# Second halves of the output sums under the slot rule, and another order at the start, in a kernel that mixes full and dilated local attention

## The chip, the cores and the metric

The kernel runs on one core of a Trainium2 chip. A core has five engines that run side by side and wait for each other on semaphores: TensorE (PE in the profile; its weight loads are PEld), VectorE (DVE), ScalarE (ACT), GpSimd (POOL) and SyncE (SP), which issues most of the transfers. The metric is the device time in microseconds (us). Before the change the median of nine runs is 851.13 us (850.04 to 852.61).

## The reference

The input x has 2048 rows of 512 numbers. Two attentions of 32 heads, 16 numbers a head, work on the same x and are mixed row by row with a gate:

```
g = sigmoid((x * gate_w).sum(-1))
A: p = softmax(q k^T / 4) over all 2048 keys;   a = (p v) @ A_wo
B: 8 keys per row, at distances 0, 2, ..., 14;  b = (softmax(q . k_w / 4) v_w) @ B_wo
out = g * a + (1 - g) * b
```

q, k and v are slices of x @ A_wqkv for A and of x @ B_wqkv for B. All in- and outputs are bf16.

## The kernel before

The work of A is cut into 32 periods, each of four heads (there are 8 groups i) and 512 queries (4 chunks c_). The list `periods` sets their order. A period has 64 units: for each of the four heads, 16 blocks of 128 keys. A unit is a score block of 128 keys by 512 queries, its exponential, and its share of the attention sums (PV). The four heads of a group sit in four strips of 32 rows, so up to four score matmuls run side by side on TensorE, and up to four PV matmuls in four strips of 32 columns.

Most units go through ScalarE. `act_stream` (L972) fills two rings in PSUM in turn, one of three score blocks and one of two, and `act_tail` (L953) takes the exponential of a whole ring in one instruction, from `ring` to `pT`. Such a ring's matmuls are called a score set here. A set can be filled again only when ScalarE has read it. Some units, called riders (`rider`, L1063), are computed elsewhere: their score block goes to one of two PSUM banks named w (`P.resource("w", 2)`, L450), and VectorE makes the exponential in four passes (ta, ta, ta, pd), or GpSimd does with psc after a copy by VectorE. `pv_job` (L892) adds the units to `acc`.

Everything else on TensorE is a job that needs a w bank: keys, queries, values, B's projections (`bw`), and the output sums. `final_job` (L1301) makes one tile of 128 output rows from eight matmuls: four with `oT` and `awo` for A, and four with `obt` and `bwo` for B, as two steps of four with the same bank (L1322; in the last chunk three, one and three). The first step has the job's priority, 30 and up, the second has `GO` = 1.9 (L471). Behind the second, VectorE copies the bank to `osb`, and SP stores it. The last of a chunk's four tiles sets `ev_final`.

No scheduler decides on the chip. The class `Plan` runs through the whole kernel once while it is built, with a cost for each step, and records the instructions in the order in which it gives them out; each engine then works through its own list. In `run` (L222) the ready step of the lowest priority number comes next on its engine. For TensorE three rules bear on the change:

- `fits` (L216): a step of priority 2 or more is held back, in steps of 0.1 us, unless its planned end lies before `limit` (L185), the planned time at which ScalarE runs out of work, less `refill` = 0.52. A step under 2 isn't asked.
- `room_for_job` (L200) and `rider` compare the work that VectorE has ahead with `JW` = 0.8: a job opens a bank only when VectorE has that much or the job has waited for 3.0 (`JP`), and riders stand back behind waiting jobs when it has more.
- `idle_fill` (L150) puts matmuls on zeros into gaps that the plan sees on TensorE (`z` by `ident` in the profile; written over a scratch bank, or added to `acc` as zeros), so that a share of 0.80 of each 3.4133 us is streamed. `stream` is told a step's length less 0.11 (L284). `SW` = 0.11 (L469) is the planned cost of going from one group of matmuls to another, `MM` = 0.2135 that of one matmul of 512 columns.

The start is in the same plan. Five transfers on SP's queue bring x (`load_x`, L395 to L403), in the order of the queue: rows 0 to 511, 512 to 1023, 1024 to 1535, and twice 256. Behind them the weights `wqr` of the first queries follow; the planned landings are `XARR` and `WARR` (L482, L483). Each quarter of x is transposed on TensorE in two halves (`x_half`, L540) and copied out by VectorE or ScalarE. `k_job` (L567) makes the keys of one quarter with four matmuls; for the first group the largest absolute key is taken by VectorE straight from the bank (`kmax_all`), and ScalarE writes the keys with a bias. `sel_job` (L598) takes the maximum of the four columns of `kmax_all` and makes the matrix `selk_all` from it. `q_job` (L750) makes the queries of a period; VectorE takes |q| (`absq`), one more matmul by `selk_all` adds a bound on the scores, and VectorE writes `qt`. Then the first score set can run. For the first period `q_job` waits for the third quarter of x (L754), though it reads the first.

## Time and profile before

| | us |
|---|---|
| median of nine runs | 851.13 |
| the profiled execution, its own time | 851.45 |
| its span, first to last instruction | 849.7 |
| TensorE busy | 758.0 |
| VectorE busy | 765.6 |
| ScalarE busy | 826.4 |
| GpSimd busy | 725.5 |
| ScalarE waiting for score sets, PE ring, 6 times | 5.1 |
| ScalarE waiting for PE acc (5 times) and PE w (3 times) | 1.6 + 1.1 |
| first exponential of a ring begins | 17.99 |
| last score set begins | 838.5 |

A row of the groups has the line, the engine, the operation, the tile written and the tile read with their shapes, the count, then the busy time in us and the mean of one in ns, and last the engine's idle time ahead of the group, with what ended it. Almost all rows name L347, the helper that records an instruction, so groups are told apart by their tiles. In a timeline a row begins with the start and the length in us; several equal instructions in succession are one row. In the table by stretches, each engine's busy time has its number of instructions behind it, and the granted TensorE clock, the DMA share and GB/s follow.

### The profile page before, as it was taken

What the parts mean: (1) busy time and instruction counts of PE and PEld (TensorE: products, weight loads), DVE (VectorE), ACT (ScalarE), POOL (GpSimd) and SP (SyncE); (2) the same over time, 40 slices, a digit from 0 to 9 for tenths busy, and PEclk for the clock granted to TensorE, in tenths of its full rate; (3) what the DMA queues carried; (4) which work ended last, traced back from release to release, by engine and by line L of the source; (5) the groups of instructions that cost most, each with busy time, mean ns of one, the idle gap of its engine ahead of it and who ended that gap; (6) DMA issues with size and microseconds to landing.
All of it is one profiled execution on the core that took longest, in us unless ns stands there. A gap on an engine that the chain in (4) does not pass through costs nothing.

```text
span 849.7 us, 15781 instructions
## 1 busy us (share of the span) xinstructions
PE 758.0 (89%) x5864; PEld 267.8 (32%) x5864; DVE 765.6 (90%) x1332; ACT 826.4 (97%) x748; POOL 725.5 (85%) x734
## 2 busy tenths in 40 slices
PE   9999999989998888888998988888898998888887
PEld 4432343333323332222333233333223223223222
DVE  5698889899999898998999899999989899999896
ACT  5999999999999999999999999999999999999996
POOL 2596886999799999899999999999899999997781
PEclk9999999999999999999999999999999999999999
DMA  9002304421444041303132414120313221201000
GB/s 295 5 14 88 100 27 140 152 64 39 129 119 162 32 127 29 112 13 105 33 93 66 124 43 130 45 94 7 106 32 112 87 81 26 63 13 57 14 1 26
DMA packets 72589, 63.84 MB, mean 75 GB/s; under 512 B 20528, under 2 KB 69168, under 8 KB 72512
## 3 DMA queue, kind: packets, MB, share of 16 engines
q1 hardware_dynamic: 71312, 62.57, 24.3%
q8 instruction: 46, 0.75, 0.4%
q10 hardware_dynamic: 1200, 0.26, 0.2%
q14 instruction: 31, 0.25, 0.1%
HBM read 46.14 MB, written 12.62 MB: 69 GB/s over the span
## 4 chain that ended last, share of the span: by engine, by line
ACT 66%; issue 20%; PE 13%; DVE 1%; POOL 0%; ACTq 0%; POOLq 0%
ACT pT L347 65%; PE w L347 5%; PE ring L347 3%; PE acc L347 3%; ACT lg L347 1%; PE s L347 1%; DVE ta L347 0%; PE e L347 0%; DVE pd L347 0%; DVE qpk L347 0%; DVE osb L347 0%; DVE kvs L347 0%; ACT osc L347 0%; ACT e L347 0%; DVE mx L347 0%
## 5 line engine op out<-in xcount | busy, mean ns | idle before, releaser
L347 ACT ACTIVATE pT<-ring 128x1536 bf16<-128x1536 f32 x717 | 816.5, 1408 | 8.0 <-PE ring L347 5.1
L347 PE MATMUL ring<-qt,kt_all 32*128 32x512 bf16 x1841 | 285.7, 381 | 82.5 <-ACT pT L347 70.0
L347 DVE SCALAR_TENSOR_TENSOR ta<-ta,w 128x512 f32<-128x512 f32 x476 | 317.3, 681 | 5.6
L347 POOL TENSOR_TENSOR prod<-prod 128x512 f32<-128x512 f32 (+1 forms) x208 | 240.3, 1166 | 5.5
L347 PE MATMUL acc<-pT,vp_all 128*17 128x512 bf16 x1793 | 221.9, 384 | 1.2 <-DVE accS L347 0.9
L347 PEld LDWEIGHTS <-kt_all 32*128 32x128 bf16 x2096 | 113.2, 91 | 335.9 <-issue 325.8
L347 PE MATMUL acc<-ident,z 128*17 128x512 bf16 (+5 forms) x773 | 198.2, 342 | 1.4 <-POOL ident masks.py:199 1.4
L347 DVE TENSOR_SCALAR ta<-w 128x512 f32<-128x512 uint16 x238 | 162.6, 686 | 37.1 <-PE w L347 35.0
L347 DVE SCALAR_TENSOR_TENSOR pd<-ta,w 128x512 uint16<-128x512 f32 x238 | 160.2, 678 | 2.5
L347 POOL TENSOR_TENSOR prod<-ksh,qb 128x512 f32<-128x512 bf16 x128 | 144.8, 1157 | 2.2
L347 POOL TENSOR_TENSOR prod<-vsh,lg 128x512 f32<-128x512 bf16 x128 | 136.7, 1097 | 2.7 <-DMA vsh<-kv_scr 0.3
L347 PE MATMUL w<-qt,kt_all 32*128 32x512 bf16 x255 | 95.6, 384 | 0.0
L347 PE MATMUL acc<-pd,vp_all 128*17 128x512 bf16 x255 | 83.4, 381 | 0.0
L347 PEld LDWEIGHTS <-z 128*17 128x17 bf16 (+1 forms) x780 | 54.3, 92 | 72.5 <-issue 44.3
L347 PEld LDWEIGHTS <-vp_all 128*17 128x17 bf16 x2048 | 40.6, 88 | 90.1 <-issue 89.9
L347 POOL TENSOR_TENSOR psc<-psc 128x512 f32<-128x512 f32 x51 | 60.9, 1194 | 3.9
L347 PE MATMUL w<-bw,xT 128*128 128x512 bf16 x192 | 49.7, 382 | 0.4
L347 POOL TENSOR_SCALAR psc<-psc 128x512 f32<-128x512 uint16 (+1 forms) x34 | 21.0, 618 | 31.9 <-DVE psc L347 29.7
L347 PEld LDWEIGHTS <-xT 128*128 128x128 bf16 x448 | 31.7, 98 | 28.8 <-issue 16.4
L347 POOL TENSOR_TENSOR lg<-lg,mx 128x256 f32<-128x256 f32 x16 | 10.1, 629 | 22.3 <-DVE mx L347 22.1
L347 DVE COPY accS<-acc 128x512 f32<-128x512 f32 (+1 forms) x33 | 21.9, 666 | 2.8 <-PE acc L347 2.7
L347 DVE CAST kvs<-w 128x512 bf16<-128x512 f32 x32 | 21.9, 684 | 0.9 <-PE w L347 0.8
(107 smaller groups left out, 453.8 us busy)
## 6 DMA issues: line engine op xcount, KB each, us to landing
ksh<-kv_scr SPq DMA_DIRECT2D x16, 1024.0 KB
vsh<-kv_scr SPq DMA_DIRECT2D x16, 1024.0 KB
kv_scr<-kvs SPq DMA_DIRECT2D x16, 256.0 KB
kt_all<-k_scr SPq DMA_DIRECT2D x6, 512.0 KB
q_scr<-qpk SPq DMA_DIRECT2D x24, 128.0 KB
qt<-q_scr SPq DMA_DIRECT2D x24, 128.0 KB
out_dram<-osb SPq DMA_DIRECT2D x14, 128.0 KB
xr<-in_A_x_dram SPq DMA_DIRECT2D x3, 512.0 KB
```

The costliest lines, as they stand in the source:

```text
L347: return chain_on(self._key, f(*a, **k))
```

## The change

It has these parts.

1. The second steps of `final_job` get priority 2.0 instead of `GO` = 1.9.
2. Numbers of the plan: `refill` 0.52 to 0.5, `JW` 0.8 to 1.6, `SW` 0.11 to 0.116, and the same 0.116 in what `stream` is told.
3. The load of the first 128 columns of `wqr` stands after the second transfer of x instead of after the fifth. `XARR` and `WARR` follow.
4. The first `q_job` waits for the first quarter of x only, and takes |q| with ScalarE instead of VectorE.
5. For the first group, the keys of the last quarter are made in two halves of 256 columns, each with its own maximum; `kmax_all` has a fifth column. `sel_job` starts when the five maxima are there, and no longer waits for ScalarE's writing of the keys.

```diff
-    refill = 0.52
+    refill = 0.5
...
-    JW = 0.8
+    JW = 1.6
...
-                    self.stream(st, x[4] - 0.11 - self.thin)
+                    self.stream(st, x[4] - 0.116 - self.thin)
...
     load_x(4, 4)
+    SP.dma_start(out=wqr[:, :, 0:128], in_=a_w3[:, :, 0:128])
     load_x(8, 4)
     load_x(12, 2)
     load_x(14, 2)
-    SP.dma_start(out=wqr[:, :, 0:128], in_=a_w3[:, :, 0:128])
...
-    SW = 0.11
+    SW = 0.116
...
-    XARR = ((5.8, 5.8), (7.2, 7.2), (8.7, 8.7), (9.4, 10.2))
-    WARR = (4.8, 11.3)
+    XARR = ((5.8, 5.8), (7.2, 7.2), (9.3, 9.3), (9.9, 10.6))
+    WARR = (4.8, 8.0)
...
-    def k_job(i, sc, rel, prio):
+    def k_job(i, sc, rel, prio, hf=None):
...
+        n = QW if hf is None else QW // 2
+        c0 = sc * QW + (hf or 0) * n
+        kc = sc + (hf or 0)
...
-            V.tensor_reduce(out=kmax_all[:, i, sc:sc + 1], in_=src, axis=AX.X, op=ALU.max, apply_absolute_value=True)
+            V.tensor_reduce(out=kmax_all[:, i, kc:kc + 1], in_=src, axis=AX.X, op=ALU.max, apply_absolute_value=True)
         if i == 0:
-            yield ("dve", prio, VP + 0.09, lambda: top(w.t[:]))
-            yield ("act", 0.5, 0.69, lambda: A.activation(out=kt, in_=w.t[:], func=ACT.Identity, bias=kbias[:, 0:1]))
+            yield ("dve", prio, 0.16 + n / 960.0, lambda: top(w.t[:]))
+            yield ("spawn", k_top(sc))
+            yield ("act", 0.5, 0.26 + n / 1200.0, lambda: A.activation(out=kt, in_=w.t[:], func=ACT.Identity,
+                                                                     bias=kbias[:, 0:1]))
...
+    halves = [2]
+    tops = [NC + 1]
+    ev_top = Event()
+
+    def k_top(sc):
+        tops[0] -= 1
+        if tops[0] == 0:
+            yield ("set", ev_top)
...
     def sel_job(i, prio):
+        if i == 0:
+            yield ("wait", ev_top)
         for sc in range(NC):
-            yield ("wait", ev_k[i][sc])
+            if i:
+                yield ("wait", ev_k[i][sc])
...
-        yield ("wait", ev_x[c_ if p else 2])
+        yield ("wait", ev_x[c_])
...
-        yield ("dve", prio, VP, absq)
+        if p == 0:
+            def absa():
+                st["a"] = work.tile([128, QW], BF16, name="absq", tag="absq", bufs=1)
+                A.activation(out=st["a"][:], in_=w.t[:], func=ACT.Abs)
+            yield ("act", 0.2, 0.69, absa)
+        else:
+            yield ("dve", prio, VP, absq)
...
-            yield ("pe", GO if a else prio, (b - a) * MM + SW, pe(a, b)) + (("w",) if a == 0 else ())
+            yield ("pe", 2.0 if a else prio, (b - a) * MM + SW, pe(a, b)) + (("w",) if a == 0 else ())
...
-    for sc in range(NC):
+    for sc in range(NC - 1):
         P.spawn(k_job(0, sc, None, 1.5))
+    for hf in range(2):
+        P.spawn(k_job(0, NC - 1, None, 1.5, hf))
```

## The prediction

> **What bounds the kernel now.** I read four views in this order: the busy shares of the page, the chain of waits, ScalarE's own waits, and the timeline around single stalls.

> ```profile
> PE 758.0 (89%) x5864; PEld 267.8 (32%) x5864; DVE 765.6 (90%) x1332; ACT 826.4 (97%) x748; POOL 725.5 (85%) x734
> L347 ACT ACTIVATE pT<-ring 128x1536 bf16<-128x1536 f32 x359 | 581.3, 1619 | 7.4 <-PE ring L347 5.1 <-PE w L347 1.1 <-PE acc L347 1.0
> L347 ACT ACTIVATE pT<-ring 128x1024 bf16<-128x1024 f32 x358 | 428.5, 1197 | 0.6 <-PE acc L347 0.6
> ```

> ScalarE (ACT) is busy for 97% of the span, nearly all of it with the exponentials pT. Its mean durations, 1619 and 1197 ns, overlap, so they are no price. The price is the spacing of their ends. In the trace it is 1.343 us for a wide one (three score blocks) and 0.917 us for a narrow one (two), 2.26 a pair, with under 0.005 us of scatter. The chain of waits shows the rhythm:

> ```profile
> 26.94 1.11 ACT pT L347
> 29.17 1.13 ACT pT L347
> 31.41 1.16 ACT pT L347
> 33.64 1.19 ACT pT L347
> ```

> One piece per pair, 2.24 apart. So the span adds up: the first exponential starts at 17.99 (head); 359 x 1.343 + 358 x 0.917 = 810.4; 16 small exponentials lg of 0.295 make 4.7 and the gate's one 0.3; stalls; the last one ends at 840.7, and the tail is 9.0. What is left for stalls is 7.4. Found one by one, as ends that came over 0.06 us later than the price after the one before, they are fifteen and sum to 7.41. (The page's idle time is less, 8.0 with 2.23 of it in the head: the overlap of 0.10 that each stall also loses isn't in it.) Beside each I read what TensorE (PE) did just before. They are of three kinds.

> First kind, 3.60 us: eight stalls at the second halves of the output sums (0.60 at 424.1, 0.40, 0.60, 0.35, 0.60, 0.44, 0.22, 0.39 at 809.9). The first of them:

> ```profile
> 422.11 0.60 PE L347 MATMUL acc<-pT,vp_all 128*17 128x512 bf16 x5
> 422.63 1.04 PE L347 MATMUL w<-bwo,obt 128*128 128x512 bf16 x4
> 423.61 0.39 PE L347 MATMUL ring<-qt,kt_all 32*128 32x512 bf16 x3
> 424.11 1.45 ACT L347 ACTIVATE pT<-ring 128x1536 bf16<-128x1536 f32 x1 [0.49 <-PE ring L347]
> ```

> Attention sums, then four matmuls of the output sum, with no score set between them: 1.50 us from 422.11 to the next scores, and the exponential waits for these.

> Second kind, 2.38 us: six stalls (99.9, 203.9, 229.5, 255.7, 409.9, 617.2) at another four-matmul job that follows a short group of attention sums. Third kind, 1.43 us at 336.8, a granted clock of half:

> ```profile
> 300.00:333.00 33.00, 28.38 (x226) 9.51 (x223) 31.71 (x55) 33.00 (x31) 31.11 (x32) 1.00 0.30 89
> 333.00:337.00 4.00, 3.71 (x19) 1.24 (x18) 3.28 (x8) 2.68 (x4) 4.00 (x4) 0.57 0.01 2
> ```

> The column after the engines is the clock: 0.57 over these 4 us. The clock record has 0.5 for 3.41 us from 333.35, the only such stretch before the end; the transposes and scores in it take about twice their time.

> **The change part by part.** The sum is made on the profiled execution: span 849.7, its own time 851.45 (1.75 around the span), the median of the runs 851.13.

> *The units.* I counted instructions in the changed program's list. Wide exponentials go from 359 to 360, narrow from 358 to 359, because VectorE's own exponentials fall from 238 to 234 and GpSimd's from 17 to 16: five score blocks move to ScalarE. The cause fits the code: a second half that waits keeps one of the two w banks for about a pair longer, and riders need a free bank. Cost: 1.343 + 0.917 = +2.26. VectorE gets 4 x 4 passes of 0.60 fewer and GpSimd one chain of 5.4 us (3 x 0.62 + 3 x 1.19); neither sets the end, so that is worth nothing.

> *Second halves* (priority GO = 1.9 to 2.0). From 2.0 on, `fits` holds the matmuls back until they end before ScalarE runs dry. In the changed list 13 of the 14 stand right behind a score set, with a score set next (score set, 4 matmuls, score set, attention sums); one has short attention sums behind it, an order charged below. The orders that stalled (attention sums and 4 or 3 matmuls in one gap, with a job in the gap before) stood 8 times before, and stalled 8 times; in the changed list there are none. The order that replaces them stood 93 times before without a stall. So -3.60. What is late next: the copy osb on VectorE, the store on SP, and the event that frees oT and obt, each a pair (2.26) later; the next user of these comes tens of us later. Ends: -3.6, and -2.6 if each new order lost 0.1.

> *SW 0.11 to 0.116, refill 0.52 to 0.5, JW 0.8 to 1.6.* These move every job. Counted by order: "short attention group, then job" before a narrow set, 4 times with 2 stalls (0.86), is there 2 times; before a wide set, 5 times with 4 stalls (1.52), once. At the same rates that leaves 0.43 + 0.30, a gain of 1.65. Against it stand orders that are rare before and more frequent now (attention sums and a transpose in one gap before a wide set, 3 to 8; job and attention sums in one gap, 1 to 3): they stalled before only under the halved clock, with about 0.02 us to spare, so I charge 0.3. Value -1.35, ends -2.1 and 0.

> *The head.* The chain before, on VectorE:

> ```profile
> 13.49 0.69 DVE L347 TENSOR_REDUCE kmax_all<-s 128x1 f32<-128x512 f32 x1 [0.17 <-PE s L347]
> 14.35 0.69 DVE L347 TENSOR_REDUCE kmax_all<-s 128x1 f32<-128x512 f32 x1 [0.17 <-PE s L347]
> 15.22 0.69 DVE L347 TENSOR_SCALAR absq<-w 128x512 int16<-128x512 int16 x1 [0.17 <-PE w L347]
> 15.82 0.14 DVE L347 TENSOR_REDUCE kmax<-kmax_all 128x1 f32<-128x4 f32 x1
> ```

> TensorE is dense from 8.9 to 15.0: keys 0.86, transposes 1.79, three keys of 0.86, the query 0.86. The change moves the query's four matmuls up ahead of the last transposes; the sum of TensorE's work is the same, so the last keys now end where the query ended, near 15.0. Behind that, absq (pace 0.60) is gone from VectorE, and the last maxima come in halves. A half on VectorE, not in the trace: between a quarter of 0.69 and the whole, near the 128x256 copies at 0.38 a piece; I take a pace of 0.35. The first half can start at 14.95 (the 0.69 before it began at 14.35, pace 0.60), the second when its matmuls are out, about 15.25; kmax at 15.62 where it was 15.82. All behind it shifts: -0.20. It is small because the last half still waits for the same TensorE end. Moved DMAs: 128 KB of query weights pass three x transfers on SP's queue; the issue costs 0.47 there, hidden, since x lands long after its issue. The landings of x (9.42, 10.17, 10.99) shift by the 0.53 that these weights took (10.99 to 11.52) to 9.96, 10.71, 11.53; TensorE now comes to them at 10.63, 11.53 and 11.98, so this too is hidden, with 0.4 left; without that cover it costs up to 0.5. ScalarE's wqp copy (0.41) fits its idle 0.42 before 9.11. The |q| on ScalarE (0.69 by the row of kt_all) fits behind kt_all at 11.4. [...] Ends for the head: -0.5, +0.7.

> *The clock.* The filler matmuls on zeros shrink: their columns sum to 301,700 before and 264,900 in the changed list, 15.3 us less at the full rate, 1.8% of the span. By row: the clock fell once with TensorE about 90% busy by the page, and cost 1.43, so thinner filling can cost more such stretches. [...] Before, the share of streaming in the 3.41 us ahead of the fall was 0.54; 4.3% of all such stretches lie under that, and 7.6% under 0.558, which is what 1.8 points less fill brings down: up to 0.8 falls more, or 1.1 us. I take half, +0.6; ends -1.4 (no fall) and +4.3 (three more).

> Sum: 2.26 - 3.60 - 1.35 - 0.20 + 0.60 = -2.29. Span 847.4, its run 849.2; against the median 848.8. The tail's list is the same, 9.0.

> **Rivals.** (1) *No fall of the clock* and the stalls as counted: -2.89 - 1.43 = -4.3, 846.8. For it: one fall only before, by an edge. Against: less filling. (2) *A new wait takes part of the gain*: x or the weights late in the head (+0.7), and the denser orders stall after all (second halves -2.6, other jobs 0): 2.26 - 2.6 + 0.7 + 0.6 = +1.0, or half of that mishap, about 850.5. For it: 0.02 us to spare in those orders. Against: TensorE is the head's bound with 0.4 to spare. (3) *Slower: the clock decides.* Without the clock term the sum is -2.89; each fall adds 1.43. To be slower by over 1.7 us takes 4.6, from the fourth additional fall on: 851.13 - 2.89 + 5.72 = 854.0. For it: 12% less filling, and a second stretch (near 767 us) streamed even less than the one that fell. Against: these did not fall. (4) *The change doesn't do what it says*: the stalls at second halves only move to other jobs, and five blocks more remain: 2.26 - 0.20 = +2.06, 853.2. Against it stand the counted orders.

> **How the numbers follow.** Told from no change is 0.2%, 1.7 us: faster is under 849.4, slower over 852.8. The likeliest case 0.58, with its own range 847.8 to 850.2: faster 0.44, same 0.14. Rival 1 0.14, faster. Rival 2 0.12: 0.03 faster, 0.09 same. Rival 3 0.10: 0.09 slower, 0.01 same. Rival 4 0.06, slower. Together 0.61, 0.24, 0.15. The range 846.8 to 851.8 leaves out rivals 3 and 4 and a little below.

> **What would show it.** After: 719 exponentials; the first at 17.8; no stall with bwo,obt ahead of it; one to two stretches of clock 0.5; stalls near 3.5 in all (0.7 + 0.3 and the clock's 2.0 to 2.5); tail 9.0. Wrong: an exponential that begins over 18.3, stalls behind jobs over 3 us, three or more falls of the clock, or the tail longer.

## The result, and the profile after

The median of nine runs after is 847.36 us (846.40 to 848.25), beside 851.20 in 29 runs of the kernel before. The ratio is 0.9954, with a 95% interval from 0.9945 to 0.9964: faster by 0.46%. The prediction was 848.8 with a range from 846.8 to 851.8. The profiled execution took 847.92, its span is 846.1.

The page of the kernel after, its busy shares and its group of all ring exponentials:

```profile
PE 748.7 (88%) x5832; PEld 267.4 (32%) x5832; DVE 754.4 (89%) x1315; ACT 828.2 (98%) x752; POOL 719.9 (85%) x728
L347 ACT ACTIVATE pT<-ring 128x1536 bf16<-128x1536 f32 x719 | 817.0, 1398 | 2.3 <-PE ring L347 1.7
```

ScalarE is busier and everyone else is less busy: five score blocks moved to it, and it idles 2.3 us ahead of its exponentials where it idled 8.0. By shape:

```profile
L347 ACT ACTIVATE pT<-ring 128x1536 bf16<-128x1536 f32 x360 | 579.4, 1609 | 1.9 <-PE ring L347 1.7
L347 ACT ACTIVATE pT<-ring 128x1024 bf16<-128x1024 f32 x359 | 425.8, 1186 | 0.4 <-PE acc L347 0.3
```

360 wide and 359 narrow ones, as counted. The wait for PE w, 1.1 us before, is gone. The rhythm in the chain of waits (start, length) is the old one, 2.24 for a pair:

```profile
23.02 1.05 ACT pT L347
25.26 1.07 ACT pT L347
```

The first output tile of the chunk, in the timeline, where before the second four matmuls stalled the exponentials by 0.60:

```profile
423.17 0.39 PE L347 MATMUL ring<-qt,kt_all 32*128 32x512 bf16 x3
423.50 1.04 PE L347 MATMUL w<-awo,oT 128*128 128x512 bf16 x4
424.47 0.39 PE L347 MATMUL ring<-qt,kt_all 32*128 32x512 bf16 x2
...
425.43 0.39 PE L347 MATMUL ring<-qt,kt_all 32*128 32x512 bf16 x3
...
425.76 1.04 PE L347 MATMUL w<-bwo,obt 128*128 128x512 bf16 x4
426.73 0.39 PE L347 MATMUL ring<-qt,kt_all 32*128 32x512 bf16 x2
```

The second four (bwo,obt) stand alone between two score sets and the attention sums have the gap before. ScalarE's exponentials run through: no stall from 422 to 428.

The same sum as in the prediction, over the two profiled executions (stalls found in the same way, as ends of exponentials over 0.06 us late):

| term | predicted | measured |
|---|---|---|
| one wide, one narrow exponential more | +2.26 | +2.26 |
| stalls at second halves, 3.60 before | -3.60 | -3.60 (none left) |
| stalls at other jobs, 2.38 before | -1.35 | -1.42 (0.43, 0.23, 0.21, 0.09 left) |
| stall under the half clock, 1.43 before | +0.60 | -1.02 (0.41 left) |
| first exponential, 17.99 before | -0.20 | +0.55 (18.54) |
| end of the last exponential to the end, 8.93 before | 0 | -0.33 (8.60) |
| sum | -2.29 | -3.56 (span 849.7 to 846.1) |

The first three terms, which were worked out from counted instructions and orders, are right to within 0.1 us. The surplus of 1.3 us is nearly the sum of the three others: the clock 1.6 better, the tail 0.3 better, the head 0.75 worse. In this pair of executions, that is: when the clock rises and falls differs from one execution of a kernel to the next (the kernel after: a rise at 6.92 and a fall at 597.42 here, 5.70 and 603.03 when it was run once more, below). A fall is called here a time at half the granted clock between the start and the tail. The clock after, by stretches (engine busy, then granted clock, DMA share and GB/s):

```profile
594.00:597.40 3.40, 2.48 (x24) 1.00 0.85 268
597.40:600.80 3.40, 3.40 (x21) 0.50 0.14 45
```

One fall as before, 3.41 us long, at 597.42. The exponentials stall behind it by 0.41, where the fall at 333.35 in the kernel before cost 1.43. Without a fall there, neither place stalls: not the second in the kernel after run once more (below; its fall came at 603.03), nor the first with the new head alone (head_only), whose list is that of before behind the head. The work ahead of the first, in before and then in head_only, at the full clock:

```profile
334.77 1.12 PE L347 MATMUL w<-identf,accS 128*128 128x128 f32 x4
335.82 0.61 PE L347 MATMUL ring<-qt,kt_all 32*128 32x512 bf16 x3
...
334.86 0.66 PE L347 MATMUL w<-identf,accS 128*128 128x128 f32 x4
335.45 0.39 PE L347 MATMUL ring<-qt,kt_all 32*128 32x512 bf16 x3
```

### The profile page after: what moved, and what is told of

Read it like the earlier page. It is cut to its first block, busy times and chain, and to the rows that moved or that the text cites. A ratio compares the mean times of both kernels' runs of the same rounds, so it can differ in the third digit from the quotient of the medians.

```text
span 846.1 us, 15708 instructions
## 1 busy us (share of the span) xinstructions
PE 748.7 (88%) x5832; PEld 267.4 (32%) x5832; DVE 754.4 (89%) x1315; ACT 828.2 (98%) x752; POOL 719.9 (85%) x728
## 4 chain that ended last, share of the span: by engine, by line
ACT 72%; issue 22%; PE 6%; POOL 0%; ACTq 0%; POOLq 0%
ACT pT L347 71%; PE acc L347 2%; PE ring L347 1%; PE w L347 1%; PE s L347 1%; ACT lg L347 1%; PE e L347 0%; ACT osc L347 0%; ACT e L347 0%; POOL ident masks.py:199 0%; POOL identf masks.py:197 0%; ACTq L347 0%; POOL ident masks.py:197 0%; POOLq L1708 0%
## 5 line engine op out<-in xcount | busy, mean ns | idle before, releaser
L347 ACT ACTIVATE pT<-ring 128x1536 bf16<-128x1536 f32 x719 | 817.0, 1398 | 2.3 <-PE ring L347 1.7
L347 PE MATMUL ring<-qt,kt_all 32*128 32x512 bf16 x1858 | 287.2, 381 | 88.4 <-ACT pT L347 70.3
L347 DVE SCALAR_TENSOR_TENSOR ta<-ta,w 128x512 f32<-128x512 f32 x468 | 312.8, 681 | 5.7
L347 POOL TENSOR_TENSOR prod<-prod 128x512 f32<-128x512 f32 (+1 forms) x208 | 240.3, 1166 | 5.7
L347 PE MATMUL acc<-pT,vp_all 128*17 128x512 bf16 x1798 | 222.6, 384 | 2.3 <-DVE accS L347 2.0
L347 PEld LDWEIGHTS <-kt_all 32*128 32x128 bf16 x2108 | 115.5, 91 | 337.6 <-issue 321.7
L347 DVE TENSOR_SCALAR ta<-w 128x512 f32<-128x512 uint16 x234 | 160.1, 686 | 41.3 <-PE w L347 39.6
L347 PE MATMUL acc<-ident,z 128*17 128x512 bf16 (+4 forms) x730 | 180.6, 333 | 1.4 <-POOL ident masks.py:199 1.4
L347 DVE SCALAR_TENSOR_TENSOR pd<-ta,w 128x512 uint16<-128x512 f32 x234 | 158.3, 679 | 2.9
L347 POOL TENSOR_TENSOR prod<-ksh,qb 128x512 f32<-128x512 bf16 x128 | 144.8, 1157 | 2.2
L347 POOL TENSOR_TENSOR prod<-vsh,lg 128x512 f32<-128x512 bf16 x128 | 136.7, 1098 | 2.4
L347 PE MATMUL w<-qt,kt_all 32*128 32x512 bf16 x250 | 94.9, 384 | 0.0
L347 PE MATMUL acc<-pd,vp_all 128*17 128x512 bf16 x250 | 83.5, 382 | 0.0
L347 PEld LDWEIGHTS <-z 128*17 128x17 bf16 (+1 forms) x732 | 50.5, 92 | 68.7 <-issue 43.7
L347 PEld LDWEIGHTS <-vp_all 128*17 128x17 bf16 x2048 | 40.7, 88 | 93.3 <-issue 92.9
L347 POOL TENSOR_TENSOR psc<-psc 128x512 f32<-128x512 f32 x48 | 57.3, 1194 | 3.6
L347 POOL TENSOR_SCALAR psc<-psc 128x512 f32<-128x512 uint16 (+1 forms) x32 | 19.8, 618 | 42.0 <-DVE psc L347 40.1
L347 PE MATMUL w<-bw,xT 128*128 128x512 bf16 x192 | 49.7, 382 | 0.2
L347 PEld LDWEIGHTS <-xT 128*128 128x128 bf16 x448 | 31.4, 98 | 28.3 <-issue 16.1
L347 POOL TENSOR_TENSOR lg<-lg,mx 128x256 f32<-128x256 f32 x16 | 10.1, 629 | 24.9 <-DVE mx L347 24.9
L347 DVE COPY accS<-acc 128x512 f32<-128x512 f32 (+1 forms) x33 | 21.9, 667 | 4.8 <-PE acc L347 4.8
L347 DVE CAST kvs<-w 128x512 bf16<-128x512 f32 x32 | 21.8, 682 | 2.3 <-PE w L347 2.3
```

What stands on the lines that cost most here:

```text
L347: return chain_on(self._key, f(*a, **k))
```

## The experiments

Twelve runs were made, one of them of the kernel after without an edit. The first four take the change apart.

**The second halves alone.** The kernel before, with priority 2.0:

```diff
-            yield ("pe", GO if a else prio, (b - a) * MM + SW, pe(a, b)) + (("w",) if a == 0 else ())
+            yield ("pe", 2.0 if a else prio, (b - a) * MM + SW, pe(a, b)) + (("w",) if a == 0 else ())
```

> The kernel before with one edit: second steps of the output sums at priority 2.0. By its list the order of attention sums and a second step in one gap, behind a job, is gone (7 before, 0 here; its last variant too); 360 wide or narrow exponentials more or less as before (359 wide, 359 narrow, one of a single block: +1.4 us). Theory (the gain is made by these stalls): stalls of the first kind 0 instead of 3.6 us, those behind short attention sums about 2.2 as before (8 such orders, 9 before), one fall of the clock; in sum 1.4 - 3.6 - 0.2 = -2.4 us, ratio 0.9972. Rival (the stalls move to other jobs): stalls stay near 7 us, +1.4 us, ratio 1.0016. Rival (the plan's numbers make the gain): under 1 us of change.

Measured: 848.82 us in 21 runs, ratio 0.9968 (0.9960 to 0.9975). No stall at a second half; seven others of 2.20 in all. ScalarE's waits (total, times, longest):

```profile
ACT pT L347 <- PE ring L347: 2.2, 1, 2.2
ACT pT L347 <- PE acc L347: 1.3, 4, 0.3
```

Before it was PE ring 5.1 in 6 times, PE acc 1.6 in 5 and PE w 1.1 in 3. The one wait of 2.2 left on a ring is the first exponential's in the head. So this part is what it was said to be, and most of the whole: its ratio is close to the 0.9972 expected.

**The numbers of the plan alone.** The kernel before, with:

```diff
-    refill = 0.52
+    refill = 0.5
...
-    JW = 0.8
+    JW = 1.6
...
-                    self.stream(st, x[4] - 0.11 - self.thin)
+                    self.stream(st, x[4] - 0.116 - self.thin)
...
-    SW = 0.11
+    SW = 0.116
```

> The kernel before with refill 0.5, JW 1.6, SW 0.116 and 0.116 in the streamed length, nothing else. By its list 359 wide and 359 narrow exponentials (+0.9 us), 12% fewer filler columns, 8 orders of a second step behind attention sums (7 before), 6 of short attention sums and a job (9 before). Theory: stalls of the first kind stay near 3.6, the second kind 1.65 instead of 2.38; 0.9 - 0.7 + 0 to 1.1 for the clock = +0.2 to +1.3 us, ratio 1.0002 to 1.0015. Rival (the plan's numbers make the gain): -2 us or more, ratio under 0.9977.

Measured: 853.28 in 7 runs, ratio 1.0037 (1.0022 to 1.0051), slower than was expected. The stalls of the first kind are there, some 4.0 us in seven places. What is new are three falls of the clock, at 253.28, 744.80 and 772.11, each 6.83 us long, with 5.65 us of stalls in and behind them. The last, by stretches:

```profile
768.80:772.20 3.40, 1.60 (x20) 0.57 (x15) 3.37 (x7) 3.40 (x5) 0.63 (x1) 0.99 0.13 39
772.20:779.00 6.80, 6.80 (x37) 1.28 (x36) 5.46 (x10) 5.74 (x5) 6.04 (x7) 0.50 0.02 4
```

TensorE, the first column, works 1.60 us of the 3.40 ahead of the fall. So the miss is the clock, and it put the question of what makes it fall.

**The head alone.** The kernel after, with parts 1 and 2 taken back:

```diff
-            yield ("pe", 2.0 if a else prio, (b - a) * MM + SW, pe(a, b)) + (("w",) if a == 0 else ())
+            yield ("pe", GO if a else prio, (b - a) * MM + SW, pe(a, b)) + (("w",) if a == 0 else ())
...
-    refill = 0.5
+    refill = 0.52
...
-    JW = 1.6
+    JW = 0.8
...
-                    self.stream(st, x[4] - 0.116 - self.thin)
+                    self.stream(st, x[4] - 0.11 - self.thin)
...
-    SW = 0.116
+    SW = 0.11
```

> The kernel before with the head's parts alone (query weights' load ahead, |q| by ScalarE, last keys' maxima in halves, with their planned landings). Same counts of exponentials and of orders as before by its list, so the steady part shouldn't differ. Theory: kmax 0.2 us earlier against the end of the last keys' matmuls, first exponential at 17.8 when the clock rises as early as in the profile of the kernel before: -0.2 us, ratio 0.9998. Rival (the head is later, as the first exponential at 18.5 in the changed kernel's profile seems to say): +0.5 us, ratio 1.0006. Rival (the clock's rise decides the head): the first exponential follows the rise of the clock, 17.8 for a rise at 5.7 and 18.5 for one at 6.9, whatever the edits.

Measured: 851.10 in 13 runs, ratio 0.9998 (0.9990 to 1.0006), no difference that can be told, nor can the -0.2 us expected. Its first exponential began at 18.65, later than the 17.99 before, with the clock rising at 7.15 instead of 5.67.

**All but the head.** The kernel before, with the edits of the first and second experiment together:

```diff
-    refill = 0.52
+    refill = 0.5
...
-    JW = 0.8
+    JW = 1.6
...
-                    self.stream(st, x[4] - 0.11 - self.thin)
+                    self.stream(st, x[4] - 0.116 - self.thin)
...
-    SW = 0.11
+    SW = 0.116
...
-            yield ("pe", GO if a else prio, (b - a) * MM + SW, pe(a, b)) + (("w",) if a == 0 else ())
+            yield ("pe", 2.0 if a else prio, (b - a) * MM + SW, pe(a, b)) + (("w",) if a == 0 else ())
```

> The changed kernel with the head's parts taken back: priority 2.0 and the plan's numbers alone. Same counts as the changed kernel by its list (360 wide, 359 narrow, no second step behind attention sums). Theory: the changed kernel's ratio 0.9954 but for 0.2 us, 0.9956; five stalls or so, 1.4 us. Rival (the head's parts matter): if they help by 1 us or more, 0.9966 or above; if they hurt by 0.5 us, 0.9948.

Measured: 847.88 in 9 runs, ratio 0.9964 (0.9954 to 0.9975). Seven stalls of 3.10; 2.23 of them come from two falls of the clock (602.6 and 769.85), 0.87 are the second kind. The ratio lies between what was expected without and with a gain from the head, and its interval holds both, so this run doesn't tell what the head is worth.

**More filling.** If thin filling made the clock fall, as the prediction's clock term says, then more filling should hold it. The kernel after, each filler longer by 128 columns behind the start, with the plan's clock and so the order of everything else unchanged:

```diff
-        d = self.filler(need, t)
+        d = self.filler(max(0.03, need + (0.0535 if self.now > 20.0 else 0.0)), t)
+        if d:
+            d = int(need * 2400.0 / 64.0) * 64 / 2400.0
```

> The changed kernel with each filler after the start 128 columns (0.053 us) longer; the plan doesn't count them, and the order of all other instructions is the changed kernel's. 324,600 filler columns instead of 278,900 (start and openings included; 317,900 in the kernel before). Theory (thinner filling lets the clock fall): falls of the clock go from one or two a run to none, mean granted clock 0.999 or more, and the time to that of the undisturbed runs, about 847.0 against 847.4. Rival (the filler itself delays the score sets): the clock holds but stalls of 0.05 appear at many sets, over 849. Rival (fillers don't decide the falls): clock and time as the changed kernel's, 0.997 and 847.4.

Measured: 848.05 in 5 runs, ratio 0.9959 (0.9947 to 0.9970). The fall is there at 597.07, and stalls of 1.66 where the kernel after had 1.37. Nothing was gained.

**Less filling.** The same with each filler shorter:

```diff
-        d = self.filler(need, t)
+        d = self.filler(max(0.03, need + (-0.10 if self.now > 20.0 else 0.0)), t)
+        if d:
+            d = int(need * 2400.0 / 64.0) * 64 / 2400.0
```

> The changed kernel with each filler after the start 192 to 256 columns (0.1 us) shorter, same order of all else; 197,500 filler columns instead of 278,900. Theory: the clock falls much more often, mean granted clock 0.98 or less, and each 0.001 costs 0.2 to 0.5 us as between the runs so far: 850 to 856. [...]

Measured: 847.65 in 6 runs, ratio 0.9958 (0.9943 to 0.9973), and again the one fall, at 597.17. The filling was cut by 29% of its columns, far more than the change took, and the clock fell no more often: the mean granted clock is .996 over the six runs, and .997 and .996 over the two sets of the kernel after. The clause "thinner filling can cost more such stretches" falls with this, in the size that the prediction gave it.

**More filling with the plan's numbers.** The numbers of the plan alone, with the longer fillers of the fifth experiment:

```diff
-        d = self.filler(need, t)
+        d = self.filler(max(0.03, need + (0.0535 if self.now > 20.0 else 0.0)), t)
+        if d:
+            d = int(need * 2400.0 / 64.0) * 64 / 2400.0
```

> The kernel with the plan's numbers alone (853.3, mean clock 0.991), with 128 columns more in each filler as above and the same order of all else. Theory (its loss is the clock): the clock back at 0.998 or more and 850.3 to 850.8, a little under the kernel before. Rival (its loss is in the stalls of its order): 852 to 853 with a full clock.

Measured: 853.69 in 12 runs, ratio 1.0026 (1.0011 to 1.0041). Falls of 6.83 us at 743.17 and 770.48, near two of the three in that kernel without the longer fillers. Neither expectation held: the clock did not come back, and the loss is not one with a full clock. So these two places seem to belong to the order of the work.

**Fewer fillers at the start.** In the head a late rise of the clock goes with a late first exponential (17.99 for a rise at 5.67 before, 18.54 for one at 6.92 after). The kernel after, with TensorE planned to be free later, which leaves out fillers ahead of the first transposes (ten of 17 are left in the profile, so seven fewer, where three were expected):

```diff
-    P.free["pe"] = 1.8
+    P.free["pe"] = 4.4
```

> The changed kernel with three fillers fewer of 512 columns ahead of the first transposes, else the same list. In the profiles these fillers run at the half clock and end at 6.3 to 7.1, with the first x landed near 5.5, and the first exponential came at 17.9 for a clock that rose by 5.7 and at 18.5 to 18.8 for one that rose near 7. Theory (the fillers hold the first transposes): transposes begin at 5.6 to 5.9, first exponential 17.2 to 17.9, about 0.6 us gained, 846.8. Rival (the fillers raise the clock): it rises later, the transposes and first keys run at half, first exponential at 18.5 or later, 847.4 to 848.5.

Measured: 848.33 in 10 runs, ratio 0.9969 (0.9958 to 0.9980). The transposes begin at 5.30 instead of 7.19, but the clock rises only at 9.95 (6.92 after), and the first exponential is at 18.77. In the timeline the transposes of a quarter's half take the longer for it, 1.89 instead of 1.07:

```profile
5.30 1.89 PE L347 MATMUL s<-ident,xr 128*128 128x128 bf16 x16 [0.88 <-DMA xr<-in_A_x_dram]
```

So the second expectation held: the fillers at the start do bring the rise of the clock forward, and what they cost comes back.

**Score sets doubled where the plan is thin.** The kernel after makes the score matmuls of a set twice near a period's end when less than 0.60 of the last 3.41 us was streamed. Here 0.72:

```diff
-    TWICE = 0.60
+    TWICE = 0.72
```

> The kernel after, with TWICE 0.60 to 0.72: where little was streamed in a stretch of 3.41 us, the plan makes the score matmuls of a set twice (45 such matmuls more in the list), so the thinnest stretches late in a period are filled with work in place. The list has 360 wide, 359 narrow and one single exponential (+0.49), and none of the orders 'short attention group, then job' that cost 0.64 in the kernel after. Theory (a fall of the clock follows a thin stretch at a fixed place of the order): no fall in the profile, mean clock .999 or more, 847.1 + 0.5 - 0.6 = 847.0 or a little less. Rival (what decides a fall is not the thinness of the stretch ahead): a fall stays, here or elsewhere, and the time is 847.4 or more. Second rival: the doubled score matmuls hold up the sets themselves, with new stalls over 1 us and 848 or more.

Measured: 852.62 in 12 runs, ratio 1.0018 (1.0001 to 1.0035). Missed on both counts. There is a fall at 553.52, and the mean clock over the twelve runs is .993. And the doubled sets hold up the exponentials themselves, by 0.64 or 0.65 in five places. One of them:

```profile
616.92 0.61 PE L347 MATMUL ring<-qt,kt_all 32*128 32x512 bf16 x6
617.46 0.60 PE L347 MATMUL acc<-pT,vp_all 128*17 128x512 bf16 x5
617.69 0.38 PE L347 MATMUL acc<-pd,vp_all 128*17 128x512 bf16 x2
618.00 0.39 PE L347 MATMUL ring<-qt,kt_all 32*128 32x512 bf16 x2
618.16 1.45 ACT L347 ACTIVATE pT<-ring 128x1536 bf16<-128x1536 f32 x1 [0.53 <-PE acc L347]
```

Six score matmuls for a set of three, behind four of a job: the set takes 0.61 where one of three takes 0.39, so the attention sums behind it begin 0.2 later, and the exponential waits, by the profile, for these. Both rivals held.

**The second halves put back.** The kernel after, with the priority alone as before:

```diff
-            yield ("pe", 2.0 if a else prio, (b - a) * MM + SW, pe(a, b)) + (("w",) if a == 0 else ())
+            yield ("pe", GO if a else prio, (b - a) * MM + SW, pe(a, b)) + (("w",) if a == 0 else ())
```

> The kernel after with the second steps at priority GO = 1.9 again. Behind the head its list is that of the plan numbers alone, only begun by the other head. Theory (falls of the clock belong to places of an order): two or three falls again, two of them near 744 and 771, the eight stalls at second halves back at about 4.0, 852.8 to 853.5. Rival (the falls of the plan numbers alone came from the old head or from chance): no more than one fall, and 847.4 + 3.6 + 0.4 - 1.0 = 850.4 or so.

Measured: 853.27 in 10 runs, ratio 1.0026 (1.0013 to 1.0039); the kernel after on the same chip (below) took 847.81. The stalls at second halves are back, 4.03 us in seven places. The first:

```profile
424.07 0.38 PE L347 MATMUL acc<-pT,vp_all 128*17 128x512 bf16 x2
424.38 1.04 PE L347 MATMUL w<-bwo,obt 128*128 128x512 bf16 x4
425.35 0.39 PE L347 MATMUL ring<-qt,kt_all 32*128 32x512 bf16 x3
425.85 1.45 ACT L347 ACTIVATE pT<-ring 128x1536 bf16<-128x1536 f32 x1 [0.49 <-PE w L347]
```

The clock falls at 486.31 and 769.61. The second is the place near 771 for the third time in this order, with another head ahead of it; the one at 744 isn't there, and 486 is new.

**The kernel after once more**, without an edit:

> The kernel after once more, beside the two others on the same chip. All theories: 847.4, one fall of 3.41 us near 597, mean clock .997 to .999.

Measured: 847.81 in 12 runs (846.44 to 853.39), ratio 0.9966 (0.9951 to 0.9982). One fall at 603.03, stalls of 1.37, span 845.5. Its clock rose at 5.70, nearly when it rose in the profile of before (5.67), which makes it the better partner for a comparison of the heads.

**What decides a fall.** By now there were thirteen traces with 16 falls. All the stretches of the clock record, from 3.41 to 839.68 us, are whole multiples of 3.4133 us, counted from the first rise, but for the last, which the end cuts off: 96, 1 and 150 of them before, 173, 1 and 72 after. So I cut each trace on its own grid, and looked for a measure of TensorE's work that sets the stretches right ahead of the falls apart. I tried seven, and the share of columns streamed, the prediction's measure, was not the best: ahead of most falls it was among the lowest three of its trace, but at three falls (before, twice72, less_fill) between seven and twenty other stretches lay lower. One measure put every fall among the lowest four of some 235 stretches in its trace: the share of the array's 128 rows in use, averaged over the stretch (a row of the profile has them ahead of the star: 32*128 is 32 rows). A matmul of 512 columns counts the plan's 0.2135 (the next one of a job begins 0.215 behind it in the profile), 16 of them fill a stretch; attention sums, jobs and fillers use all 128 rows and count 1, and sums that run side by side on the same rows count once; a score matmul uses 32 rows and counts 1/4, a set of two 1/2, of three 3/4.

How such a sum is read from a timeline, from the stretch ahead of the fall in the kernel after (594.01 to 597.42):

```profile
595.10 0.39 PE L347 MATMUL acc<-pT,vp_all 128*17 128x512 bf16 x3
595.12 0.39 PE L347 MATMUL acc<-ident,z 128*17 128x512 bf16 x1
...
596.12 0.39 PE L347 MATMUL ring<-qt,kt_all 32*128 32x512 bf16 x3 [0.42 <-ACT pT L347]
596.14 0.60 PE L347 MATMUL w<-qt,kt_all 32*128 32x512 bf16 x2
```

Three sums and a filler side by side are 1; a set of three with two riders is 1 for the four that run together and 1/4 for the fifth. With one more place of sums, a job's matmul (1 each), two sets of two (1/2 each) and what the stretch cuts off its neighbours (about 0.55) it is 5.8 of 16, or 0.36; taken from the recorded starts it is 0.380.

By this sum 15 of the 16 falls followed a stretch under 0.392 (the other 0.420), and of 3065 other stretches none lay under 0.394. Before, the fall at 333.35 followed 0.370, and the next lowest was 0.398. After, it was 0.380 and 0.406. Where the line lies depends on the way of counting: with 0.2135 from each recorded start and the fp32 transposes of accS at twice the time per column (0.11 apart in the record, where the bf16 ones of x are 0.055 apart), 15 falls are under 0.375 and no other stretch between 20 and 835 us is under 0.377. The separation is the same.

A measure picked from seven on the data that it fits proves little, so the last run changed it alone. The kernel after, with the same fillers in the same places and the same columns, but on 32 rows behind the start:

```diff
-    def filling(m):
+    def filling(m, rows=128):
...
-            return _ap(ident[:], [list(ident[:].ap[0]), [0, m // 64], [1, 64]])
-        return _ap(ident[:], [list(ident[:].ap[0]), [0, m // 128], [1, 128]])
+            return _ap(ident[0:rows], [list(ident[0:rows].ap[0]), [0, m // 64], [1, 64]])
+        return _ap(ident[0:rows], [list(ident[0:rows].ap[0]), [0, m // 128], [1, 128]])
...
-                mm(wt[0:32, 0:m], z32[:], filling(m), True, True, tile_position=(0, 0))
+                mm(wt[0:32, 0:m], z32[0:32], filling(m, 32), True, True, tile_position=(0, 0))
...
-            mm(acc_tiles[p][32 * j:32 * j + DH + 1, 0:m], z32[:, 0:DH + 1], filling(m), False, False, tile_position=(0, 32 * j))
+            mm(acc_tiles[p][32 * j:32 * j + DH + 1, 0:m], z32[0:32, 0:DH + 1], filling(m, 32), False, False, tile_position=(0, 32 * j))
```

> The kernel after, with every instruction in the same place and the same columns streamed; only the fillers behind the start use 32 of the array's 128 rows instead of all of them. Theory, formed on the thirteen traces so far: the clock is judged in stretches of 3.413 us counted from its rise, by the columns streamed times the rows in use (a 32-row score matmul counts a quarter); every one of the 16 falls ended a stretch under 0.42 of full, 15 of them under 0.392, and none of 3065 other stretches lay under 0.394. In the trace of the kernel after, a quarter of the rows in the fillers brings 41 of 237 stretches under 0.39 where one was: so tens of falls (25 to 50), mean clock .90 to .95, and at 0.3 to 0.5 us for 0.001 of clock 865 to 890. Rival (columns alone count, whatever the rows): the same one fall near 597 or 603, clock .997 to .999, 847 to 848. Second rival (what decides lies elsewhere, in other engines or chance): 847 to 850, one to three falls.

Measured: 971.97 us in 4 runs (955.23 to 986.28), ratio 1.1416 (1.1321 to 1.1511), mean clock .79 to .83. Even the fastest run is 107 us above the kernel after. From its page, TensorE's busy share with its instructions, its busy tenths in 40 slices, and the granted clock in the same slices:

```profile
PE 911.4 (96%) x5780; PEld 257.7 (27%) x5832; DVE 759.2 (80%) x1315; ACT 842.8 (88%) x752; POOL 719.2 (75%) x728
...
PE   9999999999999999999999999999999999999998
...
PEclk9999997799998989679987888785599955659776
```

Both rivals fall. There are 19 falls, fewer than the 25 to 50 expected, but many last: 317 us are run at half the clock, 93 stretches, and the longest fall takes 68 us. That at half the clock a stretch has room for only half the columns (in the fall before, the transposes of accS are 0.21 apart instead of 0.11) fits this, but no run tries it alone. The long falls are why the loss of 124 us is about three times the upper end of what I worked out from short ones. The 19 falls followed stretches of 0.328 to 0.398; of the 158 other stretches at the full clock the lowest is 0.384, and five lie under 0.398. By columns streamed the falls reach up to 0.732, and 85 other stretches lie below that.

The same place in the two kernels, by stretches, first with 32 rows:

```profile
146.30:149.76 3.46, 2.91 (x23) 1.00 0.44 136
149.76:156.59 6.83, 6.33 (x28) 0.50 0.60 215
```

and the kernel after:

```profile
146.30:149.76 3.46, 2.85 (x27) 1.00 0.44 126
149.76:156.59 6.83, 6.03 (x50) 1.00 0.62 223
```

TensorE is as busy ahead of the fall as without one (2.91 and 2.85; columns 0.60 and 0.61). Rows in use are 0.374 and 0.541. So the rows of the fillers decide here. Whether it is the rows of the weights or the data streamed into them can't be told apart, since the edit takes both from 128 to 32.

## Why the prediction was right

**The units.** +2.26 as counted. The measured spacing of ends is the same in both kernels.

**The second halves.** Right, -3.60 to the hundredth, shown from both sides: the part alone has none of these stalls, and the kernel after without it has them back. What was said to be late next cost nothing that the profile shows.

**The other jobs.** -1.42 for -1.35. The residue is made up otherwise by a little: 0.64 at "short attention group, then job" (0.43 and 0.21; 0.73 was expected), and 0.32 at the denser orders (0.23 and 0.09; 0.3 was expected). The second halves alone left 2.08 of the 2.38 (0.43 four times, 0.22, 0.14), so 0.3 of the gain comes without the new numbers.

**The head.** The step "kmax at 15.62 where it was 15.82" is right in its mechanism and mis-sized, and a term is missing ahead of it. VectorE in the kernel after:

```profile
14.11 0.69 DVE L347 TENSOR_REDUCE kmax_all<-s 128x1 f32<-128x512 f32 x1 [0.17 <-PE s L347]
14.97 1.35 DVE L347 TENSOR_REDUCE kmax_all<-s 128x1 f32<-128x512 f32 x3 [0.17 <-PE s L347]
16.36 0.16 DVE L347 TENSOR_REDUCE kmax<-kmax_all 128x1 f32<-128x5 f32 x1
```

The three maxima begin at 14.97, 15.58 and 15.91: the halves have the pace of 0.33 that was assumed (0.35). But kmax begins 0.45 behind the last half, not 0.35. It reads that half's result, while before it stood behind absq, which it doesn't read; that fits the longer step, but isn't shown to be its cause. In the run with the rise at 5.70, kmax is at 15.75, so the chain gained 0.07 there, not 0.20. The |q| on ScalarE brought no second table load: the profile after has one, of 1.28, as the profile before has. The missing term is the clock's first rise, which differs from execution to execution:

| run | head | clock rises | first transposes | first exponential | between the last two |
|---|---|---|---|---|---|
| plan_only | before | 4.11 | 5.80 | 17.92 | 12.12 |
| undo_head | before | 5.26 | 6.38 | 17.94 | 11.56 |
| before | before | 5.67 | 6.58 | 17.99 | 11.41 |
| second_only | before | 7.34 | 7.40 | 18.82 | 11.42 |
| undo_second | after | 5.03 | 6.26 | 17.60 | 11.34 |
| after_again | after | 5.70 | 6.59 | 17.94 | 11.35 |
| after | after | 6.92 | 7.19 | 18.54 | 11.35 |
| head_only | after | 7.15 | 7.30 | 18.65 | 11.35 |

From the first transposes on the new head takes 11.34 or 11.35 in all its traces but less_warm's, with transposes that begin from 6.26 to 7.40; the old one takes 0.06 more when they begin at 6.58 or later, 0.21 more at 6.38, and 0.77 more at 5.80, where no trace of the new head lies. With the early rise it has nothing to do while the third quarter of x is on its way (timeline of TensorE, numbers of the plan alone):

```profile
8.14 1.03 PE L347 MATMUL s<-xT,wkp 128*128 128x512 bf16 x3
9.45 2.21 PE L347 MATMUL s<-ident,xr 128*128 128x128 bf16 x32 [0.29 <-DMA xr<-in_A_x_dram]
```

In the new head the first query's four matmuls stand in that gap (undo_second, which has the new head):

```profile
9.46 1.03 PE L347 MATMUL w<-xT,wqp 128*128 128x512 bf16 x4
10.32 1.95 PE L347 MATMUL s<-ident,xr 128*128 128x128 bf16 x32
```

So the moved weights and landings were hidden in these traces, as the prediction said, and the gain is 0.06 at the rise of before and larger at an early rise. The +0.55 of the profiles is 0.61 of later transposes less that 0.06. "An exponential that begins over 18.3" was given as a sign that the step is wrong; it came, at 18.54, and was no such sign.

**The clock.** This is the step that was wrong in its mechanism: "thinner filling can cost more such stretches", +0.60, with the stretches ranked by the columns streamed. In these traces the falls follow rows in use. Filling matters for that (with 32 rows it cost 124 us), but the stretch ahead of the fall in the kernel after holds only two fillers, both beside attention sums that count anyway, and with 29% less filling there were no more falls.

Nor is the -1.02 of the table what the change does. It belongs to the two executions profiled. Over all executions the mean granted clock is 0.9971 in 97 runs of the kernel before, and 0.9964 in 22 of the kernel after, with a standard error of 0.0009. A line through the time of each run against its mean clock gives 0.2 to 0.6 us for 0.001 (0.04 with the longer fillers, in five runs); at 0.35 that is anything from a gain of 0.4 to a loss of 0.9. So the runs show neither a gain nor a loss by the clock, and the size of +0.60 is not refuted. The -1.02, like the head's +0.55 that takes half of it back, is the luck of which execution was profiled.

Nor do the two falls follow the longest pauses of TensorE: between 20 and 835 us the longest is 0.57 before, up to 38.63, and 0.63 after, up to 637.51, and the falls came at 333.35 and 597.42. Why falls of the same length cost 1.43 before and 0.41 after is not shown; they met other work.

At the full clock the lines give 850.5 before, 847.7 with the second halves alone, 850.0 with the numbers of the plan alone, 850.2 with the head alone, 847.1 and 846.8 for the two sets of runs after. So there the parts add up, -2.8, -0.5 and -0.3 to -3.6. Since the lines of before give 850.2 to 850.6 on four chips, the two small parts can't be told from nothing. Most of the loss of the plan's numbers alone, +2.0 on the median, is the clock in that order of work: its runs had a mean clock of .991, and its profile 5.65 us of stalls at the falls.

Without the clock, and with the head at its 0.06, the measured terms sum to 2.26 - 3.60 - 1.42 - 0.06 - 0.33 = -3.15, near those -3.6. The median came out 1.5 below the prediction: the clock's 0.60 and the tail's 0.33 account for most of what is known of it, and some 0.6 stays open. The range was wide enough for that.

**The tail.** "The tail's list is the same" holds, and still it is 0.33 shorter. For 0.2 of it, the last attention sum of a rider ran beside ScalarE's (837.68 and 837.69) where it had run behind it (840.89 and 841.11). The other 0.13 lies almost wholly behind the issue of the last store, which comes 3.56 before the end in one profile and 3.45 in the other (846.10 and 842.68).

**The rivals.** The time came out between the likeliest case and rival 1. No new wait took part of the gain (rival 2), the stalls did not move (rival 4), and the clock did not decide against the change (rival 3), though the plan's numbers alone and the doubled sets show that it can, with medians 2.0 and 1.6 us above those of the kernel before beside them.

## What to carry to other kernels

Price a stall by the order of instructions that makes it, and count these orders in the changed list: that gave -3.60 and -1.42 here, of which the last was off by 0.07. Before comparing two profiles of a few tenths of a per cent, compare when the clock rose and fell in each, since with the new head alone the first exponential came from 17.60 to 18.65 us, later the later the rise (5.03 to 7.15). Where TensorE's clock is held up by filler work, count rows in use, not columns or busy time: in this kernel 15 of 16 falls to half the clock followed a stretch of 3.41 us with under 0.392 of the array's rows in use, and the same fillers on 32 rows brought the granted clock down to .79 to .83.
